# Projected K transposed by a crossbar DMA, the first two batches' attention in another order, and a split last output tile, in a fused attention and feed-forward kernel

## The chip, the cores and the metric

The kernel runs on one core of one Trainium2 chip. The metric is the device time of one execution in microseconds (us), the median of several runs. A core has five engines that run in parallel: TensorE (PE in the profile, its weight loads PEld), VectorE (DVE), ScalarE (ACT), GpSimd (POOL), and SyncE (SP). SP and POOL do no arithmetic here; they issue DMAs. The profile counts the DMAs of both queues as shares of the same 16 DMA engines (36.1% and 16.0% of the span before). PSUM is the memory that PE writes its results to; from there another engine has to copy them out, which is called an eviction.

## The reference, cut to what matters

```python
# q, k, v: (8 batches, 8 heads, 1024 tokens, 64) float32; E, F: (64, 1024); w_in: (512, 2048); w_out: (2048, 512)
k_proj = einsum('ks,bhsd->bhkd', E, k)          # keys projected from 1024 tokens to 64
v_proj = einsum('ks,bhsd->bhkd', F, v)
attn   = softmax(q @ k_proj.T / 8)              # 1024 x 64 for each head
x      = concat_heads(attn @ v_proj)            # 8192 x 512
out    = relu(x @ w_in) ** 2 @ w_out            # 8192 x 512
```

For the scores PE needs the projected K of a batch with the head's 64 features on the partitions. The projection leaves the 64 projected keys there, so K has to be transposed, and so has Q. Below, kp is a batch's projected K, kT the transposed kp and qT the transposed Q. A crossbar transpose is a DMA that transposes what it moves.

## The kernel before

The kernel walks over eight batches. The feed-forward part of batch b is cut into 64 steps (four matmuls of 128x512 each, 0.86 us), and the attention of batch b+1 and the projection of batch b+2 are threaded between these steps. PE's program order is fixed by hand. The order on the other engines and on the DMA queues is chosen by a scheduler when the program is built.

```python
def project(self):                      # K and V of one batch, on PE, into one PSUM bank
    ...
    self.keep_k(ps[LO, :])              # two VectorE copies: kp is [64 keys, 8 heads, 2, 64]
def transpose_k(self, h=slice(0, 8)):   # on PE: 8 transposes of 64x128, then one copy out of PSUM
    ...
    nc.vector.tensor_copy(self.kT[:, h], ps[:, h])
def transpose_q_dma(self):              # Q of batches 2 to 7: 1 MB transposed by a DMA
    nc.sync.dma_start_transpose(self.qT[:]..., self.Q[:]...)
def store(self, c, tb, ps):             # one output tile, on the same Sync queue
    nc.scalar.copy(o[:], ps[:]); nc.sync.dma_start(out_rows[...], o[:])
# ... loads: K, V, Q are double-buffered, issued on POOL's queue; weights are loaded once;
#     Q0's second half is the last load before batch 1's
# ... plan, batch 0: Q0's transposes at steps 19 and 20, batch 1's attention from step 36 on,
#     at(60, coming.project); at(62, coming.transpose_q_dma); at(64, coming.transpose_k)
# ... plan, other batches: at(14, nxt.scores, 0) and so on,
#     at(27, coming.transpose_q_dma); at(30, coming.project); at(49, coming.transpose_k)
```

The softmax here doesn't subtract the row's maximum and nothing guards it: scores larger than these inputs give would overflow.

## Time and profile before

| | |
|---|---|
| time, median of 3 runs | 522.35 us (522.2 to 522.53) |
| span of the profiled run | 521.1 us |
| PE busy | 506.3 us (97%) |
| one batch in the steady part | 61.2 us |
| PE idle for Q0's second half | 2.9 us, once |
| PE idle for a PSUM buffer (scores of batch 1) | 2.0 us in two waits |

The page of the profile, parts 1 and 2: busy time of each engine with its share of the span, then the span in 40 slices of 13 us (a digit is the busy share in tenths; PEclk is the clock that was granted to PE), and the chain of work that ended last.

```profile
PE 506.3 (97%) x2764; PEld 223.8 (43%) x2764; DVE 174.7 (34%) x367; ACT 287.1 (55%) x428; POOL 32.2 (6%) x44
PE   7897999999999999999999999999999999999997
PEclk9899999999999999999999999999999999999999
DMA  9999999999995099104851050110101011010102
PE 90%; DMA 7%; POOL 1%; ACT 1%; DVE 0%; issue 0%; POOLq 0%
```

PE bounds the kernel, except in the first slices, and the DMA engines are full for 12 slices, that is to 156 us. The waits of PE in the kernel before (who waited for whom, us in total, how often, longest):

```profile
PE ps_bank L216 <- DMA Q_sb<-in_q_dram: 2.9, 1, 2.9
PE ps_att L241 <- ACT rs L260: 2.0, 2, 1.0
```

Now the Sync queue. Timeline of the kernel before, three engines and the Sync queue (start us, duration us, engine, line, operation, out<-in, count): an output tile is copied out of PSUM by ACT at 83.40; POOL issues batch 3's and batch 4's Q loads when batch 2's Q transpose has freed the buffer; the Sync queue (SPq) issues batch 3's Q transpose and only then six stores; PE starts batch 2's scores.

```profile
83.40 0.58 ACT L340 COPY o_sb<-ps_bank 128x512 f32<-128x512 f32 x1 [0.33 <-PE ps_bank L333]
...
91.94 1.75 POOL L76 DMA_DIRECT2D Q_sb<-in_q_dram  x2 [27.61 <-DMA qT<-Q_sb]
...
102.18 7.46 SPq L233 DMA_TRANSPOSE qT<-Q_sb  x1
109.69 10.89 SPq L342 DMA_DIRECT2D out_dram<-o_sb  x6
...
109.35 0.63 PE L241 MATMUL ps_att<-qT,kT 64*64 64x512 bf16 x8
111.65 1.03 PE L333 MATMUL ps_bank<-w_out_124,hsq 128*128 128x512 bf16 x4
```

The tile of 83.40 us leaves at 109.69. The queue is worked off in order: while its head, batch 3's Q transpose, waits for a load, everything behind it waits too. Here that cost nothing, since nobody waited for the stores. Why that load is late can be read from the built program: batch 3's Q goes into the buffer of batch 2's Q, so its load is issued only at 91.94 us, when batch 2's transpose has read that buffer; the other buffer, last read by PE's transposes of batch 1's Q, which start by 73.0 us, goes to batch 4's Q.

### The profile page before, as it was taken

The numbers are of one execution on the slowest core, as the hardware profiler recorded it, in microseconds if no ns is written. First come the engines' busy times: TensorE is split into PE (matmuls) and PEld (weight loads), VectorE is DVE, ScalarE is ACT, GpSimd is POOL, SyncE is SP. The second block draws the span as 40 slices with busy tenths as digits, with TensorE's granted clock in tenths as the row PEclk, the third lists the DMA queues.
The fourth block names the chain that finished last, engine by engine and source line by source line (L and its number), as shares of the span: only waits on it lengthen the run. The fifth ranks groups of instructions, "written<-read, shape, count | busy, mean of one in ns | idle before, by whom it ended". The sixth has DMA issues, their size and how long they took to land.

```text
span 521.1 us, 6860 instructions
## 1 busy us (share of the span) xinstructions
PE 506.3 (97%) x2764; PEld 223.8 (43%) x2764; DVE 174.7 (34%) x367; ACT 287.1 (55%) x428; POOL 32.2 (6%) x44
## 2 busy tenths in 40 slices
PE   7897999999999999999999999999999999999997
PEld 3443443444444444444444444444444444444443
DVE  2351552433513244142431325232440424313130
ACT  1563475574735667276654756356662766544351
POOL 6420100120200020000100000000000000000000
PEclk9899999999999999999999999999999999999999
DMA  9999999999995099104851050110101011010102
GB/s 154 205 205 206 241 207 186 135 207 206 185 191 127 25 179 202 69 13 79 170 97 60 1 142 21 40 42 20 62 1 60 21 40 42 20 62 20 62 0 81
DMA packets 64975, 53.26 MB, mean 102 GB/s; under 512 B 26416, under 2 KB 56624, under 8 KB 64944
## 3 DMA queue, kind: packets, MB, share of 16 engines
q0 software_dynamic: 30880, 29.49, 36.1%
q1 hardware_dynamic: 34064, 23.34, 16.0%
q8 instruction: 21, 0.34, 0.3%
q14 instruction: 10, 0.08, 0.1%
HBM read 59.24 MB, written 16.78 MB: 146 GB/s over the span
## 4 chain that ended last, share of the span: by engine, by line
PE 90%; DMA 7%; POOL 1%; ACT 1%; DVE 0%; issue 0%; POOLq 0%
PE ps_bank L333 43%; PE ps_bank L327 40%; DMA Q_sb<-in_q_dram 4%; DMA w_in_116<-in_moe_w_in_dram 3%; PE ps_bank L182 2%; PE ps_att L247 2%; PE ps_att L241 2%; PE ps_att L281 1%; PE ps_bank L281 0%; PE ps_bank L206 0%; ACT rs L260 0%; POOL Q_sb L76 0%; POOL K_sb L76 0%; POOL V_sb L76 0%; PE ps_bank L216 0%
## 5 line engine op out<-in xcount | busy, mean ns | idle before, releaser
L323 ACT ACTIVATE h_relu<-ps_bank 128x512 bf16<-128x512 f32 x256 | 151.3, 599 | 63.7 <-PE ps_bank L327 62.8
L324 DVE TENSOR_TENSOR hsq<-h_relu 128x512 bf16<-128x512 bf16 x256 | 108.8, 425 | 195.0 <-ACT h_relu L323 193.7
L333 PEld LDWEIGHTS <-hsq 128*128 128x128 bf16 x1024 | 97.6, 98 | 123.2 <-issue 9.3
L340 ACT COPY o_sb<-ps_bank 128x512 f32<-128x512 f32 x64 | 37.3, 586 | 114.8 <-PE ps_bank L333 114.8
L333 PE MATMUL ps_bank<-w_out_128,hsq 128*128 128x512 bf16 x256 | 65.7, 380 | 0.0
L333 PE MATMUL ps_bank<-w_out_124,hsq 128*128 128x512 bf16 x256 | 65.6, 379 | 0.0
L333 PE MATMUL ps_bank<-w_out_126,hsq 128*128 128x512 bf16 x256 | 65.6, 379 | 0.0
L333 PE MATMUL ps_bank<-w_out_130,hsq 128*128 128x512 bf16 x256 | 65.4, 379 | 0.0
L327 PE MATMUL ps_bank<-xT,w_in_122 128*128 128x512 bf16 x256 | 59.2, 379 | 0.0
L327 PE MATMUL ps_bank<-xT,w_in_118 128*128 128x512 bf16 x256 | 58.2, 379 | 0.1
L327 PE MATMUL ps_bank<-xT,w_in_120 128*128 128x512 bf16 x256 | 58.0, 379 | 0.0
L260 ACT ACTIVATE rs<-ps_att 128x1024 f32<-128x1024 f32 x32 | 32.7, 1024 | 23.2 <-PE ps_att L247 23.1
L327 PEld LDWEIGHTS <-w_in_120 128*128 128x128 bf16 x256 | 25.0, 98 | 30.4 <-issue 0.4
L327 PEld LDWEIGHTS <-w_in_118 128*128 128x128 bf16 x256 | 24.9, 98 | 30.1 <-issue 0.4
L327 PEld LDWEIGHTS <-w_in_122 128*128 128x128 bf16 x256 | 24.4, 98 | 30.8 <-issue 2.7
L255 ACT ACTIVATE expT<-ps_att 128x1024 bf16<-128x1024 f32 x32 | 31.8, 1023 | 10.1 <-PE ps_att L241 10.1
L285 DVE TENSOR_TENSOR xT<-ps_att,rs 128x512 bf16<-128x512 f32 x32 | 20.6, 686 | 44.6 <-ACT rs L261 44.6
L261 ACT ACTIVATE rs<-rs 128x1024 f32<-128x1024 f32 x32 | 33.8, 1059 | 0.6
L285 DVE TENSOR_TENSOR xT<-ps_bank,rs 128x512 bf16<-128x512 f32 x24 | 15.5, 686 | 50.5 <-ACT rs L261 50.5
L327 PE MATMUL ps_bank<-xT,w_in_114 128*128 128x512 bf16 x128 | 30.6, 379 | 1.1 <-DVE xT L310 1.1
L327 PE MATMUL ps_bank<-xT,w_in_116 128*128 128x512 bf16 x128 | 30.4, 379 | 0.0
L327 PEld LDWEIGHTS <-w_in_114 128*128 128x128 bf16 x128 | 12.4, 98 | 16.1 <-issue 1.7
(64 smaller groups left out, 203.5 us busy)
## 6 DMA issues: line engine op xcount, KB each, us to landing
out_dram<-o_sb SPq DMA_DIRECT2D x64, 256.0 KB, 2.0
K_sb<-in_k_dram POOLq DMA_DIRECT2D x7, 1024.0 KB, 17.9
V_sb<-in_v_dram POOLq DMA_DIRECT2D x7, 1024.0 KB, 23.7
Q_sb<-in_q_dram POOLq DMA_DIRECT2D x7, 1024.0 KB, 10.8
K_sb<-in_k_dram POOLq DMA_DIRECT2D x2, 512.0 KB, 8.0
V_sb<-in_v_dram POOLq DMA_DIRECT2D x2, 512.0 KB, 12.0
Q_sb<-in_q_dram POOLq DMA_DIRECT2D x2, 256.0 KB, 8.3
w_in_118<-in_moe_w_in_dram POOLq DMA_DIRECT2D x1, 512.0 KB, 15.1
```

The source lines that it names most:

```text
L182: nc.tensor.matmul(ps[LO, :], lhsT=ET[:, i, :], rhs=self.K[:, :, i, :], start=f, stop=l)
L241: nc.tensor.matmul(ps[o, par], lhsT=self.kT[r, h, :], rhs=self.qT[r, h, n, :], start=True, stop=True)
L247: nc.tensor.matmul(ps[o, par], lhsT=ones[r, :], rhs=e[r, par], start=True, stop=True)
L255: nc.scalar.activation(e[:], ps[:], AF.Exp, scale=SCALE)
L260: nc.scalar.activation(rs[:], ps[:], AF.Ln)
L261: nc.scalar.activation(rs[:], rs[:], AF.Exp, scale=-1.0)
L285: nc.vector.tensor_tensor(out=self.xT[:, pr, :, par], in0=ps_x[par].rearrange("p (c t) -> p c t", c=2), in1=rs[:, par].rearrange("p (c t) ...
L323: nc.scalar.activation(r[:], ps[:], AF.Relu)
L324: nc.vector.tensor_tensor(out=self.hsq[c][:, fb, :], in0=r[:], in1=r[:], op=ALU.mult)
L327: nc.tensor.matmul(ps[:], lhsT=w_in_blk(cb, fb), rhs=self.xT[:, cb, c].rearrange("p a t -> p (a t)"), start=(cb == 0), stop=(cb == NCB - 1),)
L333: nc.tensor.matmul(ps[:], lhsT=self.hsq[c][:, fb, tb * P:(tb + 1) * P], rhs=w_out_blk(fb), start=(fb == 0), stop=(fb == NFB - 1),)
L340: nc.scalar.copy(o[:], ps[:])
```

## The change

Its intent is to relieve PE: the transposes of K leave it, the waits of the first two batches are spaced away, and the last store becomes smaller. Cut to its core:

```diff
 # loads: Q0's second half one place earlier
     for j in range(WP):
+        if j == WP - 1:
+            load(Q0[:, :, 4:8, :], tokens(q, 0, i=slice(4, 8)))
         t = wpool.tile([P, fn, DM], BF16, name=f"w_out_{j}")
...
-    load(Q0[:, :, 4:8, :], tokens(q, 0, i=slice(4, 8)))
 # K: four head pairs on 128 partitions (four VectorE copies), transposed by the DMA for batches 2 to 7
-            self.kp = proj_pool.tile([KP, H, 2, D], BF16, name="kp")
+            self.kp = proj_pool.tile([P, H // 2, 2, D], BF16, name="kp")
+        def transpose_k_dma(self):
+            nc.sync.dma_start_transpose(
+                self.kT[:].rearrange("p j g k -> p j (g k)"), self.kp[:].rearrange("p j a d -> p (j a d)")
+            )
 # last tile of the last batch in two column halves, each with its own copy and store
+                            for m in (slice(0, DM // 2), slice(DM // 2, DM)):
+                                ps = bank()
+                                for fb in range(NFB):
+                                    self.second_mm(c, tb, fb, ps, m)
+                                self.store(c, tb, ps, m)
 # start: another order, 22 dummy matmuls instead of 12 (cut)
 # plan of batch 0: Q0's transposes at step 20; batch 1's stages respaced, three of four with spare banks
-                    at(36, nxt.transpose_q, 0)
+                    at(37, nxt.transpose_q, 0)
...
-                        at(60, coming.project)
-                        at(62, coming.transpose_q_dma)
-                        at(64, coming.transpose_k)
+                        at(61, coming.project)
+                        at(63, coming.transpose_q_dma)
+                        at(62, coming.transpose_k_dma)
 # plan of batches 1 to 5
-                        at(s5, coming.transpose_k)
+                        at(31, coming.transpose_k_dma)
```

The diff doesn't show the order in which the scheduler put the DMAs on the Sync queue. It can be read from the built program. "waits" are semaphores; DVE stands for the copies that make kp, DMASW1 for batch 3's Q load.

```
before                                    after
qT of batch 2                             qT of batch 2
qT of batch 3   (waits DMASW1, ...)       qT of batch 3   (waits DMASW1, ...)
store, tile 4 of batch 0                  store, tile 4 of batch 0
store                                     store
store                                     store
store                                     kT of batch 2   (waits DVE, ...)
store                                     store
```

More of the change, by code (lines that the diff above doesn't have):

```diff
@@ L155, in __init__ @@
             self.xT = x_pool.tile([P, NCB, 2, 2, HC], BF16, name="xT")
-            self.kp = proj_pool.tile([KP, H, 2, D], BF16, name="kp")
-            self.kT = proj_pool.tile([P, H, KP], BF16, name="kT")
+            self.kp = proj_pool.tile([P, H // 2, 2, D], BF16, name="kp")
+            self.kT = proj_pool.tile([P, H // 2, 2, KP], BF16, name="kT")
             self.vp = proj_pool.tile([P, H, D], BF16, name="vp")
@@ L164, in load, with keep_k, keep_v @@
             return first
-        def keep_k(self, ps_k, h=slice(0, 8), second=None):
+        def keep_k(self, ps_k, g, second=None):
             view = ps_k.rearrange("k (h d) -> k h d", d=D)
-            nc.vector.tensor_copy(self.kp[:, h, 0, :], view)
-            (second or nc.vector.tensor_copy)(self.kp[:, h, 1, :], view)
-        def keep_v(self, ps_v, h=slice(0, 8)):
+            rows = (LO, HI)[g]
+            nc.vector.tensor_copy(self.kp[rows, :, 0, :], view)
+            (second or nc.vector.tensor_copy)(self.kp[rows, :, 1, :], view)
+        def keep_v(self, ps_v, h=slice(0, 8), first=None):
             view = ps_v.rearrange("k (h d) -> k h d", d=D)
-            nc.scalar.copy(self.vp[HI, h], view)
+            (first or nc.scalar.copy)(self.vp[HI, h], view)
             nc.vector.tensor_copy(self.vp[LO, h], view)
@@ L183, in project @@
                 nc.tensor.matmul(ps[HI, :], lhsT=FT[:, i, :], rhs=self.V[:, :, i, :], start=f, stop=l)
-            self.keep_k(ps[LO, :])
+            for g in range(2):
+                self.keep_k(ps[LO, g * C // 2:(g + 1) * C // 2], g)
             self.keep_v(ps[HI, :])
@@ L192, in project_k @@
                 )
-            self.keep_k(ps[LO, 0:C // 2], half[g], nc.scalar.copy)
+            self.keep_k(ps[LO, 0:C // 2], g, nc.scalar.copy)
         def project_v(self, g):
@@ L200, in project_v, with transpose_k @@
                 )
-            self.keep_v(ps[HI, 0:C // 2], half[g])
-        def transpose_k(self, h=slice(0, 8)):
-            ps = bank([P, H, KP], BF16)
-            for hh in range(h.start, h.stop):
+            self.keep_v(ps[HI, 0:C // 2], half[g], nc.vector.tensor_copy)
+        def transpose_k(self, gs=(0, 1)):
+            ps = bank([P, H // 2, 2, KP], BF16)
+            rows = slice((LO, HI)[gs[0]].start, (LO, HI)[gs[-1]].stop)
+            g = slice(gs[0], gs[-1] + 1)
+            for j in range(H // 2):
                 nc.tensor.transpose(
-                    ps[:, hh, :], self.kp[:, hh].rearrange("k a d -> k (a d)"), ident[0:KP, 0:KP]
-                )
-            nc.vector.tensor_copy(self.kT[:, h], ps[:, h])
+                    ps[:, j, g, :].rearrange("p g k -> p (g k)"),
+                    self.kp[rows, j].rearrange("k a d -> k (a d)"), ident[rows, rows]
+                )
+            nc.vector.tensor_copy(self.kT[:, :, g], ps[:, :, g])
+        def transpose_k_dma(self):
+            nc.sync.dma_start_transpose(
+                self.kT[:].rearrange("p j g k -> p j (g k)"), self.kp[:].rearrange("p j a d -> p (j a d)")
+            )
         def transpose_q_chunk(self, c, src, hg):
@@ L241, in scores_mm @@
                 nc.tensor.matmul(
-                    ps[o, par], lhsT=self.kT[r, h, :], rhs=self.qT[r, h, n, :], start=True, stop=True
+                    ps[o, par], lhsT=self.kT[r, h % 4, h // 4, :], rhs=self.qT[r, h, n, :], start=True, stop=True
                 )
@@ L330, in first_mm, with second_mm, store @@
             )
-        def second_mm(self, c, tb, fb, ps):
+        def second_mm(self, c, tb, fb, ps, m=slice(0, DM)):
             nc.tensor.matmul(
-                ps[:], lhsT=self.hsq[c][:, fb, tb * P:(tb + 1) * P], rhs=w_out_blk(fb),
+                ps[:, m], lhsT=self.hsq[c][:, fb, tb * P:(tb + 1) * P], rhs=w_out_blk(fb)[:, m],
                 start=(fb == 0), stop=(fb == NFB - 1),
             )
-        def store(self, c, tb, ps):
+        def store(self, c, tb, ps, m=slice(0, DM)):
             o = out_pool.tile([P, DM], F32, name="o_sb")
-            nc.scalar.copy(o[:], ps[:])
+            nc.scalar.copy(o[:, m], ps[:, m])
             i = 2 * (2 * c + tb % 2) + tb // 2
-            nc.sync.dma_start(out_rows[self.b, i, :, :], o[:])
+            nc.sync.dma_start(out_rows[self.b, i, :, m], o[:, m])
         def steps(self):
@@ L377, in steps @@
                 else:
+                    last = self.b == B - 1 and c == 1
                     for tb in range(4):
+                        if last and tb == 3:
+                            for m in (slice(0, DM // 2), slice(DM // 2, DM)):
[3 more added lines that the diff above has]
+                                self.store(c, tb, ps, m)
+                            break
                         ps = bank()
@@ L389 @@
         nc.vector.tensor_copy(e_bf[:], e_f32[:])
-        warm(4)
+        warm(8)
         ET = projection("ET", e_bf)
-        warm(8)
+        warm(3)
         att = Attention(0)
@@ L395 @@
         att.transpose_q_chunk(0, Q0, 0)
-        att.transpose_k(half[0])
+        att.transpose_k((0,))
+        warm(1)
         att.chunk_scores(0, 0)
+        warm(2)
         att.project_k(1)
+        att.chunk_sums(0, 0)
         att.transpose_q_chunk(0, Q0, 1)
-        att.chunk_sums(0, 0)
-        att.transpose_k(half[1])
+        att.transpose_k((1,))
+        warm(1)
         att.chunk_scores(0, 1)
         FT = projection("FT", f_bf)
+        warm(3)
+        att.chunk_sums(0, 1)
         att.project_v(0)
-        att.chunk_sums(0, 1)
+        warm(2)
         att.chunk_values(0, 0)
+        warm(2)
         att.project_v(1)
@@ L417 @@
                 at(2, att.chunk_values, 0, 1)
-                at(19, att.transpose_q_chunk, 1, Q0, 0)
+                at(20, att.transpose_q_chunk, 1, Q0, 0)
                 at(20, att.transpose_q_chunk, 1, Q0, 1)
@@ L433 @@
                     at(36, nxt.project)
-                    at(36, nxt.transpose_q, 0)
-                    at(36, nxt.transpose_q, 1)
+                    at(37, nxt.transpose_q, 0)
+                    at(37, nxt.transpose_q, 1)
                     at(39, nxt.transpose_k)
-                    s1, s2, s3, s4, s5 = 42, 47, 50, 55, 60
-                    at(44, nxt.transpose_q, 2)
-                    at(45, nxt.transpose_q, 3)
-                else:
-                    s1, s2, s3, s4, s5 = 14, 18, 24, 30, 49
@@ L442 @@
-                at(s1, nxt.scores, 0)
-                at(s1, nxt.scores, 1)
-                spare = b > 0
-                at(s2, nxt.values, 0, spare)
-                at(s2, nxt.scores, 2)
-                at(s3, nxt.values, 1, spare)
-                at(s3, nxt.scores, 3)
-                at(s4, nxt.values, 2)
-                at(s5, nxt.values, 3)
+                    at(41, nxt.scores, 0)
+                    at(41, nxt.scores, 1)
+                    at(43, nxt.transpose_q, 2)
+                    at(43, nxt.transpose_q, 3)
@@ new lines @@
+                    at(45, nxt.values, 0)
+                    at(49, nxt.scores, 2)
+                    at(51, nxt.values, 1, True)
+                    at(51, nxt.scores, 3)
+                    at(55, nxt.values, 2, True)
+                    at(59, nxt.values, 3, True)
+                else:
+                    at(14, nxt.scores, 0)
+                    at(14, nxt.scores, 1)
+                    at(18, nxt.values, 0, True)
+                    at(18, nxt.scores, 2)
+                    at(24, nxt.values, 1, True)
+                    at(24, nxt.scores, 3)
+                    at(30, nxt.values, 2)
+                    at(49, nxt.values, 3)
@@ L451 @@
                 if b + 2 < B:
                     if b == 0:
-                        at(60, coming.project)
-                        at(62, coming.transpose_q_dma)
-                        at(64, coming.transpose_k)
+                        at(61, coming.project)
+                        at(63, coming.transpose_q_dma)
+                        at(62, coming.transpose_k_dma)
                     else:
-                        at(s4, coming.project)
+                        at(30, coming.project)
```

## The prediction

> What bounds it now. TensorE (PE): the page has it busy 506.3 of 521.1 us, and the chain of waits is 90% PE. From batch 1 on it never waits (windows: 13.00 busy of 13.00); a batch costs 61.2 us. PE's idle time lies in the first 27 us (DMA-bound: loads of 1 MB read land every 2.6 us and the chain runs through them), in 2.9 us before the transposes of Q0's second half (PE idle 39.7 to 42.57, wait list "Q_sb 2.9"), in 2.0 us where scores wait for a PSUM buffer (wait list "ACT rs 2.0, 2 times", near 76 and 81 us), and in the 3.6 us tail (last matmul 517.5, copy 0.58, store).
>
> What the change removes, by the timeline's durations:
> - Q0's load one place earlier: lands about 2.6 us sooner; -2.9 us.
> - New spacing and spare banks in batch 0: up to -2.0 us.
> - K's transposes on PE: 8 in 0.34 us, six times, and half of one batch's: -2.2 us. Their evictions and the extra K copies (four of 0.42 instead of two of 0.68) are on VectorE, 34% busy: free.
> - Last tile in halves: copy about 0.37 instead of 0.58, smaller last store: -0.3 us.
> - The dummy matmuls and the reordered start: about 0; w_in's second piece lands at 22.07 whatever PE does.
> Alone that would give about 515 us.
>
> What it adds. The order of instructions puts batch 2's kT transpose on the Sync queue behind batch 3's Q transpose and three stores. That queue is in order: in the trace of before, an output tile copied at 83.4 us is stored only at 109.69, because the queue sat behind that Q transpose, which waits for its Q load to land (102.18) and then takes 7.46 us to issue. The load in turn waits for batch 2's Q transpose (issued 76.02, done about 91.9) to free its buffer. All of this is DMA-limited from the start and does not move when PE gets ahead. So kT of batch 2 is issued at about 109.7 + 3 x 0.47 = 111.1 us and lands, by an estimate from the Q transposes (4.13 us for eight times the bytes, 1.6 us from issue's end to landing), at 113.3 to 114.5.
> PE needs it for batch 2's first scores, step 14 of batch 1: at 109.35 us before, at about 104.0 after the savings above. So PE should stand still for about 10 us, and the savings before it are lost. By the Trainium skill (TensorE: Matmul & The Clock Gate, Part 1) an idle window of about 3.4 us halves the clock until one busy window has passed; [...]the 2.9 us gap cost no clock. I take 2.4 us for that.
>
> Sum: scores at about 113.7 instead of 109.35: +4.3; clock +2.4; five kT transposes left -1.7; tail -0.3. 522.35 + 4.7 = 527.0 us; range 523.0 to 530.5. Faster by over 2%: 0.01; within 2%: 0.94; slower: 0.05.
>
> Right if: the wait list shows one wait of 8 to 12 us of PE's weight load or matmul for DMA kT near 104 to 114 us; the chain of waits runs through Q_sb, qT and kT by DMA there; granted clock falls to about half just after; the Q_sb wait of 2.9 is under 0.7; later batches take about 60.85 us with no kT wait; the tail after the last matmul is shorter than 3.6 us.
>
> Wrong if: kT lands before PE asks (then about 515); batch 3's Q load lands earlier; the clock stays up or recovers at once (about 524.5); a kT or Q transpose of a later batch is late too (above 530).

## The result, and the profile after

The changed kernel takes 526.47 us (median of 4 runs, 526.11 to 527.03) against 522.36 us for the kernel before. The ratio is 1.008 (95% interval 1.0062 to 1.0097). Ratios here are the mean time of one kernel's fast runs over that of the other's of the same rounds, so not quite the ratio of the medians.

Parts 1 and 2 of the page, and the chain, of the changed kernel:

```profile
PE 506.2 (96%) x2738; PEld 223.7 (43%) x2738; DVE 174.4 (33%) x377; ACT 286.1 (55%) x427; POOL 32.1 (6%) x44
PE   7799999939999999999999999999999999999997
PEclk9999999969999999999999999999999999999999
PE 86%; DMA 11%; SPq 1%; POOL 1%; issue 1%; ACT 0%; POOLq 0%; ACTq 0%
```

One slice, the ninth, has PE at 3 and the clock at 6 tenths. PE's busy time has hardly moved although it has fewer instructions, partly because some of them ran at half clock, partly because 22 dummy matmuls (7.8 us) stand where there were 12 (5.5 us). The waits of PE after:

```profile
PE ps_att L253 <- DMA kT<-kp: 8.3, 1, 8.3
PE ps_bank L185 <- ACT o_sb L352: 0.6, 1, 0.6
PE ps_bank L238 <- DMA Q_sb<-in_q_dram: 0.4, 1, 0.4
PE ps_bank L228 <- DMA Q_sb<-in_q_dram: 0.3, 1, 0.3
```

The old waits are nearly gone (Q0's is the 0.3), and one of 8.3 us is new. The Sync queue and PE of the changed kernel around it:

```profile
101.43 7.28 SPq L245 DMA_TRANSPOSE qT<-Q_sb  x1
108.75 1.55 SPq L354 DMA_DIRECT2D out_dram<-o_sb  x3
110.39 1.22 SPq L219 DMA_TRANSPOSE kT<-kp  x1
...
103.03 1.89 PE L339 MATMUL ps_bank<-xT,w_in_122 128*128 128x512 bf16 x8
113.19 1.07 PE L253 MATMUL ps_att<-qT,kT 64*64 64x512 bf16 x8 [8.28 <-DMA kT<-kp]
114.19 3.50 PE L339 MATMUL ps_bank<-xT,w_in_122 128*128 128x512 bf16 x8
117.53 1.03 PE L345 MATMUL ps_bank<-w_out_124,hsq 128*128 128x512 bf16 x4
```

PE is through with its work at 104.92, 4.4 us earlier than before (109.35), and then stands until kT of batch 2 lands. It had been ready to be transposed since the copies at about 92 us. The first w_out matmuls behind it start 5.88 us later than before (117.53 against 111.65): 3.84 us of that are the scores' later start (113.19 against 109.35), the other 2.04 us are the clock. The windows of the changed kernel show it (stretch, its length, busy us and instruction count of PE, PEld, DVE, ACT, POOL, then the granted clock, DMA share, GB/s):

```profile
104.00:108.00 4.00, 0.92 (x5) 0.20 (x2) 1.13 (x3) 1.19 (x2) 0.00 (x0) 0.90 1.28 171
108.00:112.00 4.00, 0.00 (x0) 0.00 (x0) 0.00 (x0) 0.00 (x0) 0.74 (x1) 0.50 1.18 347
114.00:116.00 2.00, 2.00 (x9) 0.71 (x6) 0.00 (x0) 1.83 (x2) 0.00 (x0) 0.50 0.99 164
118.00:120.00 2.00, 2.00 (x19) 0.71 (x17) 0.42 (x1) 0.52 (x2) 0.00 (x0) 1.00 1.25 208
```

From there to the end the changed kernel wins back 2.0 us (5.88 - 3.9, where 3.9 is the difference of the spans, 525.0 and 521.1): a batch takes 60.84 us instead of 61.2, and 3.3 instead of 3.6 us pass from the last matmul's end to the end of the span.

### The profile page after: what moved, and what is told of

Same layout as the page of the kernel before. It is cut to its first block, busy times and chain, and to the rows that moved or that the text cites. A ratio compares the mean times of both kernels' runs of the same rounds, so it can differ in the third digit from the quotient of the medians.

```text
span 525.0 us, 6847 instructions
## 1 busy us (share of the span) xinstructions
PE 506.2 (96%) x2738; PEld 223.7 (43%) x2738; DVE 174.4 (33%) x377; ACT 286.1 (55%) x427; POOL 32.1 (6%) x44
## 4 chain that ended last, share of the span: by engine, by line
PE 86%; DMA 11%; SPq 1%; POOL 1%; issue 1%; ACT 0%; POOLq 0%; ACTq 0%
PE ps_bank L345 40%; PE ps_bank L339 39%; DMA Q_sb<-in_q_dram 8%; DMA w_in_122<-in_moe_w_in_dram 3%; PE ps_bank L185 2%; PE ps_att L259 2%; PE ps_att L253 1%; SPq L245 1%; PE ps_bank L293 1%; PE ps_att L293 1%; DMA kT<-kp 1%; PE ps_bank L238 0%; POOL K_sb L76 0%; SPq L354 0%; ACT rs L272 0%
## 5 line engine op out<-in xcount | busy, mean ns | idle before, releaser
L345 PEld LDWEIGHTS <-hsq 128*128 128x128 bf16 x1040 | 99.1, 98 | 124.6 <-issue 10.6
L352 ACT COPY o_sb<-ps_bank 128x512 f32<-128x512 f32 (+1 forms) x65 | 37.5, 579 | 110.8 <-PE ps_bank L345 110.8
L345 PE MATMUL ps_bank<-w_out_128,hsq 128*128 128x512 bf16 (+1 forms) x260 | 65.8, 376 | 0.0
L345 PE MATMUL ps_bank<-w_out_124,hsq 128*128 128x512 bf16 (+1 forms) x260 | 65.8, 376 | 0.0
L345 PE MATMUL ps_bank<-w_out_126,hsq 128*128 128x512 bf16 (+1 forms) x260 | 65.6, 376 | 0.0
L345 PE MATMUL ps_bank<-w_out_131,hsq 128*128 128x512 bf16 (+1 forms) x260 | 65.6, 376 | 0.0
L297 DVE TENSOR_TENSOR xT<-ps_bank,rs 128x512 bf16<-128x512 f32 x30 | 19.3, 686 | 60.7 <-ACT rs L273 60.7
L339 PEld LDWEIGHTS <-w_in_122 128*128 128x128 bf16 x256 | 24.8, 99 | 32.8 <-issue 4.9
L339 PEld LDWEIGHTS <-w_in_120 128*128 128x128 bf16 x256 | 24.9, 98 | 30.1 <-issue 0.4
L339 PEld LDWEIGHTS <-w_in_118 128*128 128x128 bf16 x256 | 24.9, 98 | 29.9 <-issue 0.4
L297 DVE TENSOR_TENSOR xT<-ps_att,rs 128x512 bf16<-128x512 f32 x26 | 16.8, 686 | 38.6 <-ACT rs L273 38.6
L253 PE MATMUL ps_att<-qT,kT 64*64 64x512 bf16 (+1 forms) x144 | 11.7, 373 | 8.8 <-DMA kT<-kp 8.3
```

The source lines that it names most:

```text
L253: nc.tensor.matmul(ps[o, par], lhsT=self.kT[r, h % 4, h // 4, :], rhs=self.qT[r, h, n, :], start=True, stop=True)
L297: nc.vector.tensor_tensor(out=self.xT[:, pr, :, par], in0=ps_x[par].rearrange("p (c t) -> p c t", c=2), in1=rs[:, par].rearrange("p (c t) ...
L339: nc.tensor.matmul(ps[:], lhsT=w_in_blk(cb, fb), rhs=self.xT[:, cb, c].rearrange("p a t -> p (a t)"), start=(cb == 0), stop=(cb == NCB - 1),)
L345: nc.tensor.matmul(ps[:, m], lhsT=self.hsq[c][:, fb, tb * P:(tb + 1) * P], rhs=w_out_blk(fb)[:, m], start=(fb == 0), stop=(fb == NFB - 1),)
L352: nc.scalar.copy(o[:, m], ps[:, m])
```

## The experiments

Theory: batch 2's kT is late only because of its place in the Sync queue, behind a Q transpose that waits for its load; the wait then also halves the clock. Rivals: the crossbar transpose is itself slow or starved; the slow matmuls after the wait have another cause; the parts of the change simply add up. Three chips served the three groups of runs, and on the later ones the kernel before varied more (522.2 to 524.9 us) than in the first measurement, so ratios to the kernel before of the same rounds are used.

### Only the issue order repaired

```diff
         def transpose_k_dma(self):
-            nc.sync.dma_start_transpose(
+            k_dma[self.b] = nc.sync.dma_start_transpose(
...
         def transpose_q_dma(self):
+            with tc.issue_after(k_dma[2].ins) if self.b == 3 else nullcontext():
                 nc.sync.dma_start_transpose(
```

> Edit: nothing but the issue order on the Sync queue; batch 3's Q transpose is queued behind batch 2's K transpose (an order of issue, no added wait for data). Queue-order theory: batch 2's kT is issued as soon as K's copies are done (about 92 us) and lands before PE asks for it at 104.8 us, even if contention makes it take 10 us; the 8.3 us wait and the half clock after it vanish; the time is the changed kernel's minus about 8.4 minus 2.2 = about 515.5 us (514.5 to 517), faster than both kernels. Rival (the crossbar transpose itself is slow or starved by the loads then in flight, whatever its place in the queue): kT lands after 105 us again and the time stays above 520.

Measured: 516.9 us (516.15 to 517.54) against 524.0, ratio 0.9872 (0.9848 to 0.9895): faster than both kernels, by 1.3% than the kernel before. There is no wait for kT. The Sync queue and PE of this kernel:

```profile
88.35 1.54 SPq L357 DMA_DIRECT2D out_dram<-o_sb  x3
91.52 1.21 SPq L221 DMA_TRANSPOSE kT<-kp  x1
101.34 17.83 SPq L248 DMA_TRANSPOSE qT<-Q_sb  x1
...
104.66 0.63 PE L256 MATMUL ps_att<-qT,kT 64*64 64x512 bf16 x8
```

kT is issued at 91.52, as soon as kp is there. Part of the rival is true: with the loads of Q in flight it took 9.5 us to land, against 2.76 in the changed kernel. But it lands at 101.0, 3.7 us before PE asks. The same transpose, issued 19 us earlier, makes the difference of about 10 us, so the order is the cause. One side effect: the rebuilt program also issues batch 4's K and V loads earlier on POOL's queue (at 92.57 and 93.44 us, in the changed kernel from 112 us on). In the next experiment they stay at 112 us and the time is the same, so they do not make the difference.

The other way out, to issue kT from ScalarE's queue, was not tried. The Trainium skill (DMA: Bandwidth & Descriptors, DMA Transpose (X-bar), the part on silent corruption) says that two streams of DMA transposes in flight at once can corrupt each other's output; kT would run beside Q's transposes from the Sync queue. No run here tests that.

### Batch 2's K alone back on PE

```diff
-                        at(62, coming.transpose_k_dma)
+                        at(64, coming.transpose_k)
```

> Edit: batch 2's K alone is transposed on PE (step 64 of batch 0, as before the change), the other five stay with the DMA. Both theories about the queue agree that the wait goes: PE pays four transposes, about 0.22 us, plus the eviction wait if any; 515.7 us (514.7 to 517.2), so within 0.1% of the kernel with the order repaired. If the loss has another cause (a later batch, the split last tile, the half clock from elsewhere) the time stays near 526.

Measured: 517.2 us, ratio 0.9877 (0.9855 to 0.9899), scores of batch 2 at 105.81 us without a wait. One batch of six carries the whole loss. The fault of the change can be taken away on either side, the queue or the user of the queue.

### Q0's second half loaded last again

```diff
-        if j == WP - 1:
-            load(Q0[:, :, 4:8, :], tokens(q, 0, i=slice(4, 8)))
...
+    load(Q0[:, :, 4:8, :], tokens(q, 0, i=slice(4, 8)))
...
-                at(20, att.transpose_q_chunk, 1, Q0, 0)
+                at(19, att.transpose_q_chunk, 1, Q0, 0)
```

> Edit: the changed kernel with Q0's second half loaded last again and its transposes at step 19 again (this part of the change undone). If what PE gains before batch 2's first scores is lost in the wait for kT, the time does not move: 526.5 us (within 0.6), the wait for Q0 of 2.9 us comes back and the wait for kT shrinks by as much, to about 5.4 us. If the parts simply add, it is 2.9 us slower: 529.4.

Measured: 527.45 us, ratio 1.0067 (1.0038 to 1.0096), against 1.008 and, in a later group, 1.0064 for the whole change. Undoing this part does not move the time, as the theory had it, and the rival that the parts add up is out: it would need a ratio of about 1.012 to 1.014 (an estimate: 1.0064 or 1.008, plus the 2.9 us of Q0's wait). The time lies 0.35 us above the range that was expected, in rounds in which the kernel before took 524.0 us. Waits of PE in this run:

```profile
PE ps_att L252 <- DMA kT<-kp: 6.4, 1, 6.4
PE ps_bank L193 <- DMA K_sb<-in_k_dram: 1.8, 1, 1.8
PE ps_bank L227 <- DMA Q_sb<-in_q_dram: 0.9, 1, 0.9
```

The wait for kT shrinks, to 6.4 us. The wait for Q0 shows 0.9 and not 2.9, because the start of this run was 2.4 us later (the first w_out matmul at 39.54 us instead of 37.14); so the shift between the two waits is seen, but not in the sizes that were expected.

### PE kept busy while it waits

```diff
+                    if b == 1:
+                        at(14, warm, 36)       # 36 matmuls on zeros, results unused
                     at(14, nxt.scores, 0)
```

> Edit: the changed kernel with 36 dummy matmuls (zeros, about 7.8 us in all at full clock) put just before batch 2's first scores, so that PE is busy while it would have waited. Theory that the idle time halved the clock: the granted clock stays at 1.00 from 104 to 118 us, the scores and the eight matmuls behind them take 0.56 and 1.73 us instead of 1.07 and 3.43, and the time falls by about 2.2 us to 524.3. If the slow matmuls after the wait have another cause (the transposes or loads in flight), the time stays at 526.5.

Measured: 525.0 us (524.09 to 525.46), ratio 1.0025 (1.0002 to 1.0048), about 0.4% under the whole change. PE and the windows of this kernel:

```profile
104.84 7.93 PE L145 MATMUL ps_bank<-zeros 128*128 128x512 bf16 x35
113.64 0.63 PE L253 MATMUL ps_att<-qT,kT 64*64 64x512 bf16 x8 [0.86 <-DMA kT<-kp]
114.19 1.90 PE L339 MATMUL ps_bank<-xT,w_in 128*128 128x512 bf16 x8
...
108.00:112.00 4.00, 4.00 (x21) 1.80 (x19) 0.00 (x0) 0.00 (x0) 0.32 (x1) 1.00 1.20 331
114.00:116.00 2.00, 2.00 (x17) 0.87 (x10) 0.00 (x0) 1.90 (x3) 0.30 (x1) 1.00 0.92 129
```

The scores start at about the same time (113.64), the clock stays at 1.00, and the eight matmuls behind the scores take 1.90 instead of 3.50 us. So the 2 us behind the wait are the clock's, as the Trainium skill (TensorE: Matmul & The Clock Gate, Part 1) lets one expect of an idle PE, and not a matter of the DMAs in flight, which were nearly the same (347 GB/s from 108 to 112 us in the changed kernel, 331 here).

### K's part alone, twice

The kernel before with K of batches 2 to 7 transposed by the DMA, in the new layout, and nothing else.

```diff
-                        at(64, coming.transpose_k)
+                        at(64, coming.transpose_k_dma)
...
-                        at(s5, coming.transpose_k)
+                        at(31, coming.transpose_k_dma)
```

> Edit: the kernel before with one part of the change alone, K of batches 2 to 7 transposed by the DMA (and the layout of kp and kT that this needs). In the built order batch 2's kT stands behind batch 3's Q transpose and three stores here too. Queue-order theory: kT of batch 2 lands at about 113 to 114.5 us whatever PE did before; PE asks at about 109.0, waits 4 to 5.5 us, and the clock falls if an idle window fits in (2.2 us more); total 525.5 to 527.5 us, the same as the whole change within 0.3%, because what the rest of the change gains comes before that wait. If the parts add, it is the changed kernel plus the 5 us of the other parts, about 531; if the DMA is free, 520.3.

Measured: 530.19 us, ratio 1.0129 (1.0099 to 1.016). This was a miss: the part alone is slower than the whole change, and close to what the adding-up rival had said. It was therefore run again next to the unaltered changed kernel on one chip.

> The changed kernel unaltered, a yardstick on the same chip for the run of K's part alone: it was measured on another chip than the experiments. Expected as before, 1.008 of the kernel before (1.006 to 1.010), with one wait for kT of 7 to 9 us and the half clock behind it.

> K's part alone once more, same chip as the whole change. It came out 2.6 us slower than the whole change, where a kT that lands at the same moment in both should give the same total. Theory A (kT's landing is set by the DMA chain alone; the first run fell on a slower chain, kT took 4.0 instead of 2.8 us to land): kT lands within 1 us of the whole change's and the totals agree within 1 us. Theory B (PE's lead does move the landing, or more clock is lost): it is again 2 to 3.5 us slower than the whole change on the same chip; then the trace should show kT landing 2 to 3 us later, or a longer stretch at half clock.

Measured: the whole change 526.36 us, ratio 1.0064 (1.0044 to 1.0084); K's part alone 530.06 us, ratio 1.0121 (1.0102 to 1.014). The difference is real: 0.57%, 3.0 us. Sync queue of the whole change first, then of K's part alone, same chip:

```profile
101.19 6.96 SPq L245 DMA_TRANSPOSE qT<-Q_sb  x1
108.20 1.54 SPq L354 DMA_DIRECT2D out_dram<-o_sb  x3
109.84 1.22 SPq L219 DMA_TRANSPOSE kT<-kp  x1
```

```profile
101.74 8.56 SPq L242 DMA_TRANSPOSE qT<-Q_sb  x1
110.35 1.53 SPq L351 DMA_DIRECT2D out_dram<-o_sb  x3
111.98 1.23 SPq L216 DMA_TRANSPOSE kT<-kp  x1
```

In the profiled runs kT releases PE at 114.83 us in K's part alone and at 112.66 in the whole change. From there to the end of the span both take 412.1 us (526.9 - 114.83 and 524.8 - 112.66). So the profiled difference of 2.1 us is there when kT lands and does not grow afterwards. What follows is not the same in every part: the third group of matmuls after the release starts 6.55 us behind it in the whole change and 5.99 us in K's part alone, so the clock costs the whole change 0.56 us more, which it wins back later. (The profiled run of K's part was its fastest; the others took up to 1.6 us more, and in the first group's trace kT came at 116.14.) And the adding-up rival is right by accident: the wait for Q0 is in this trace (2.9 us), but the wait for kT, 6.0 us, still covers it. What fails is the assumption that the chain of DMAs runs alike in both kernels. It ran 2.1 us later here, 0.55 us up to the landing of batch 3's Q and 1.6 in the time its transpose took to issue (8.56 against 6.96). Why is open: PE's progress and the order of the loads both differ. The moment also scatters from trace to trace: 112.66, 113.19 and 113.64 us in three traces with the changed start and schedule, 114.83 and 116.14 in the two of K's part alone. The first transpose of this queue, batch 2's, took 12.6 to 13.0 us to issue in seven traces with the changed kernel's start and schedule and 13.4 to 14.0 in six without them, but 13.4 also in the one run below with only the old start.

### K's part alone, with the issue order repaired

> K's part alone with the one-line repair of the issue order. Queue-order theory: no wait for kT; what is left is the gain that the part was made for, six times 0.34 us of PE: the kernel before minus 2.0 us, ratio 0.996 (0.994 to 0.998). If the crossbar transposes disturb the loads or Q's transposes, it is no faster than before.

Measured: 522.25 us, ratio 0.9974 (0.9956 to 0.9992). The same edit as in the first experiment turns K's part from a loss of 1.2% into a gain of 0.26%, about 1.4 us. The expected 2.0 us lie within the interval. So in this run the DMA transposes cost less than they save.

### Everything but the DMA for K

```diff
-                        at(62, coming.transpose_k_dma)
+                        at(64, coming.transpose_k)
...
-                        at(31, coming.transpose_k_dma)
+                        at(49, coming.transpose_k)
```

> Edit: the changed kernel with all of K transposed on PE (in the new layout, four transposes of 128 by 128 a batch instead of eight of 64 by 128), everything else kept. No wait for kT: about 516.5 us by five more batches of four transposes (0.22 us each) than the kernel with batch 2 alone on PE; range 515.7 to 518. It says what the DMA for K is worth once nothing waits for it: about 1.1 to 1.3 us, 0.25%.

Measured: 517.61 us, ratio 0.9891 (0.9871 to 0.9912). No wait for kT. Nearly all the gain is in the parts that had nothing to do with the DMA for K. What the DMA for five batches adds, 0.9877 against 0.9891, is about 0.7 us, but the two ratios come from two chips and their intervals overlap: its sign agrees, its size isn't settled.

### The last tile alone, and Q0's load alone

> Edit: the kernel before with the last output tile in column halves alone. Predicted minus 0.3 us: the last copy 0.37 instead of 0.58 us and a last store of half the bytes, against 16 more matmuls of 256 columns that cost PE 3.49 instead of 3.46 us. Expect 0.1 to 0.4 us less than the kernel before, which five rounds may just not tell from nothing; the trace should have 3.3 us from the last matmul's end to the end of the span instead of 3.6.

Measured: 522.41 us, ratio 0.9982 (0.9964 to 1.0). A gain, if any, of at most 0.36%; five rounds do not tell the expected 0.3 us from nothing. In its trace 3.2 us pass from the last matmul's end to the end of the span, against 3.6 before.

The edit of the other run is the reverse of that in "Q0's second half loaded last again", made in the kernel before.

> Edit: the kernel before with Q0's second half loaded one place earlier and its transposes at step 20 alone. In the kernel before nothing waits for kT, so the gain should arrive whole: the 2.9 us wait for Q0 gone (under 0.7), 519.5 us (519 to 520.3), against no movement at all when the same part was undone in the changed kernel.

Measured: 521.21 us (520.53 to 522.42), ratio 0.996 (0.9938 to 0.9982): 2.1 us faster, in the kernel in which nothing waits for kT. The contrast with the third experiment holds, but 2.9 us was too much, and the waits of PE in this run say why:

```profile
PE ps_att L242 <- ACT rs L261: 2.0, 2, 1.0
PE ps_bank L227 <- DMA Q_sb<-in_q_dram: 1.7, 1, 1.7
```

The line number is that of batch 1's transposes: PE now comes for batch 1's Q at 59.45 us, before its load has landed (61.18). The wait for Q0 is gone, and 1.7 us of it come back as a wait for the next load of the same full DMA queue. The changed kernel asks for that load one step later (step 37) and waits only 0.4 us. That is presumably what the respacing there is for; no run tests it alone.

### The old start

The kernel with the repaired order, with the order of stages and the dummy matmuls of the first 20 us as before the change.

> The changed kernel with the order repaired, and the first 20 us as before the change (old order of the stages, the old 12 dummy matmuls instead of 21). If the start is bound by the loads, as the prediction had it, this costs nothing: 516.9 us within 0.8, though the granted clock falls to about 0.85 in places from 14 to 21 us; the first matmuls with the third piece of w_in start at 26.6 to 27.0 us in both. If the dummies matter it is 1 us or more slower.

Measured: 516.06 us, ratio 0.9869 (0.985 to 0.9888), against 0.9872 with the new start. The start costs and gains nothing that can be seen. (The expectation says 21 dummy matmuls; the changed kernel has 22.) One detail missed: in this run's profile the clock did not fall at all between 12 and 22 us.

## Why the prediction was right

It was right: 527.0 us forecast, 526.47 measured, within 523.0 to 530.5, and for the stated reason. Point by point:

- kT's moment. Forecast 113.3 to 114.5 us; PE was released at 113.19. Issue was forecast at 111.1 and was 110.39. From there the forecast leaves 2.2 to 3.4 us to the landing, and 2.80 us passed until PE was released (issuing kT took 1.22 us, where an eighth of Q's 4.13 would have been 0.52). That an issue 0.7 us too early and a longer transfer than the low end of the estimate cancelled is luck; the mechanism does not rest on it.
- PE's moment. Forecast 104.0 us, measured 104.9. The savings before it were 4.4 us and not 5.4. In the trace two new waits add up to the missing microsecond: 0.4 us is the wait for batch 1's Q and 0.6 a wait for a PSUM bank behind an output copy (L185 on ACT o_sb); the run with Q0's part alone shows the first of these at full size.
- The wait. Forecast about 10 us, 8 to 12 as the sign to look for; measured 8.3.
- The clock. Forecast 2.4 us; 2.04 us by the traces, and keeping PE busy through the wait kept the clock at 1.00.
- What comes later. Forecast 1.7 + 0.3 us; measured 2.0 together. A batch takes 60.84 us (forecast 60.85).
- "Alone that would give about 515 us." With the order repaired the ratio is 0.9872, which on 522.36 is 515.7.
- "All of this is DMA-limited from the start and does not move when PE gets ahead." This sentence was too strong. On one chip kT landed 2.1 us later in the kernel whose PE was further behind; what moved it stays open. The first moment of landing was hit in part by luck: the chain of the changed kernel happened to run close to that of the kernel before.

## What to carry to other kernels

A DMA queue is a program of its own: before moving work onto it, read from the built program what it will stand behind, and what the thing ahead of it waits for. A wait behind such a queue swallows every gain made before it on the waiting engine, and one that leaves PE idle can cost clock on top (the waits of 5.7 us and more for kT did; of the waits of 2.5 to 2.9 us for Q0, two did and three did not), so the parts of a change cannot be judged by adding them up. If a wait goes away on a full DMA queue, look for it at the next load.

## What the Trainium skill lacked or had wrong

- DMA: Bandwidth & Descriptors does not say what becomes of the DMAs that are queued on the Sync queue behind one whose data isn't there yet. Here they waited: a finished output tile from 84.0 to 109.69 us behind a Q transpose, and one line of issue order was worth about 2% (ratios 1.008 and 0.9872).
- The same page gives bandwidths for DMA transposes (261 GB/s, and about 350 to 400 in the contiguous case), but not how far the time depends on company and size. 128 KB (kT) landed 2.3 to 12.0 us after issue within one run, and 1 MB (qT) 5.7 to 19.2 us in the kernel before, the longest ones beside loads. From issue to landing that is at best about 184 GB/s for qT (an estimate: 1 MB in 5.7 us).
- TensorE: Matmul & The Clock Gate, Part 1, says that the clock drops after at least one idle window of about 3.4 us. Here less idle time was enough: the clock fell 2.3 to 3.5 us after PE's last matmul in five traces (seen in windows of 0.5 us) and came back 3.2 to 5.1 us after PE restarted, and in the kernel before it fell at 17.2 us with no gap of PE over 0.53 us in the 8 us before. A wait of 2.86 us for Q0 cost the clock in one run of K's part alone (0.50 from 42.2 to 45.6 us) and not in the profiled run of the kernel before. The same page calls the window free-running, and the stretches at half clock agree with that: they lasted 3.41, 6.83 and 10.24 us in three traces, whole multiples of 3.41, so the same wait may or may not cost clock. What the traces do not bear out is that the window has to be idle throughout.
- The same page, Part 4, gives about 275 ns for a transpose on PE in a kernel's context and says that full clock doesn't engage for transposes. Here 16 of 128x128 in a row took 0.90 us from the first start to the next matmul (62.09 to 62.99 us before), 56 ns each, at a granted clock of 1.00; 219 ns is the single one's duration. They stood among other matmuls, so whether transposes alone would keep the clock is not shown.
